# The last sequence chunk's bias in whole-array products, and the opening steps in an order written by hand

## The chip, the cores and the metric

One core of a Trainium2 chip runs the whole program in one launch. The metric is device time in microseconds (us) of an execution, the median of several; times of single steps come from one profiled execution. The engines are TensorE (PE, with its weight loads as PEld), VectorE (DVE), ScalarE (ACT), GpSimd (POOL) and SyncE (SP), which issues the transfers.

## The reference

Attention with a bias from a small network on relative positions, then an MLP with a squared ReLU (B = 4, H = 8, S = 576, D = 64, hidden 32):

```python
scores = scale * np.matmul(q, k.transpose(0, 1, 3, 2))
rel = (pos[:, None] - pos[None, :]).astype(np.float32)
psi_rel = np.log1p(np.abs(rel))
psi_i = np.log1p(np.maximum(pos[:, None].astype(np.float32), 1.0))
x = (psi_rel / psi_i)[..., None]
h = np.maximum(x @ w1 + b1, 0.0)
bias = h @ w2                                  # (S, S, H)
scores = scores + bias.transpose(2, 0, 1)[None]
attn = softmax(scores);  y = attn @ v          # (B, H, S, D)
x = y.transpose(0, 2, 1, 3).reshape(2304, 512)
g = np.maximum(x @ w_in, 0.0) ** 2
out = g @ w_out
```

## The kernel before, in words

**The bias.** It is the same for all batches. A hidden unit is either on or off, and for a row i it switches at one distance, theta[unit, i]. So a 0/1 mask (distance >= theta) is made by DVE for 32 hidden units by 4 positions on the 128 partitions, and a product with the small matrix `wmov` (w1*w2 and b1*w2, in two fp16 parts, scaled by a power of two) sums the units on PE. The result has a part to be multiplied by x (`xc`, on DVE) and a part to be added (scaled on ACT); POOL adds the two into `bias_t`, slices of the large tile `area`.

**Chunks.** The 576 rows are four chunks of 128 rows and a tail of 64 (`TAIL`, index 4). One head fills the partitions in a full chunk; in the tail, two heads share them, 64 rows each. The columns j come in blocks of 32 (`jb`, 18 of them). For a full chunk a block takes one mask of 128 x 8 x 128 and 16 products of 128 mask columns by 64 columns of `wmov` (L378). For the tail a block covers 64 columns of j: one mask holds the 64 rows for two neighbouring 32-column pieces, and 64 products of 64 mask columns by 32 columns (L397) put each head pair's half on its own partitions. There are nine such blocks.

**Opening.** The transfers of col (w1, b1, w2, psi of the tail), dist, psi, xc and the first keys, queries and values are issued by SP. PE runs 12 products of ones to warm up. `bias_scalars`, `bias_signs`, `bias_exp`, `bias_theta` make theta for the tail's 64 columns and for the main 512 with DVE steps, an exponential and a logarithm on ACT; `bias_weights` makes `wmov` on DVE, with one small product (pw) that finds the power of two. Then the tail's nine blocks follow, for which three mask buffers exist, and the loads of the further heads. The order of all this is chosen by a scheduler from a modelled timeline.

**Units.** The first 40 units (8 tail units, then 8 for each chunk) are pairs of heads of two batches: score products (L429), a DVE step that subtracts the bias and takes the minimum (L439), the exponential on ACT (L444), transposes, products with the values (L528). A line in that loop has the bias blocks for the next chunk done meanwhile, 20 of chunk 0's and the next one's by the eighth tail unit. This part is scheduled by the same planner; from unit 40 on, and in the MLP, the order is written by hand.

Of the kernel before, what the change touches and what calls it, by code (L numbers as in the profile page):

```python
# [77 lines left out]
def attention_then_relu2_mlp(ctx: ExitStack, tc: tile.TileContext, q, k, v, cols, w_in, w_out, psi, xmat, dist, out):  # L78
# [205 lines left out]
    def bias_scalars():  # L284
        ts = DVE.tensor_scalar
        ts(out=iz, in0=w1, scalar1=0.0, scalar2=None, op0=ALU.is_equal)
        DVE.tensor_tensor(out=den, in0=w1, in1=iz, op=ALU.add)
        DVE.reciprocal(out=den, in_=den)
        DVE.tensor_tensor(out=tt, in0=b1, in1=den, op=ALU.mult)
        ts(out=tt, in0=tt, scalar1=-1.0, scalar2=50.0, op0=ALU.mult, op1=ALU.min)  # L290
        ts(out=tt, in0=tt, scalar1=-50.0, scalar2=None, op0=ALU.max)

    def bias_signs():
        ts = DVE.tensor_scalar
        ts(out=pos, in0=w1, scalar1=0.0, scalar2=None, op0=ALU.is_gt)
# [5 lines left out]
        DVE.tensor_tensor(out=tmp, in0=tmp, in1=iz, op=ALU.mult)
        DVE.tensor_tensor(out=kk, in0=neg, in1=sg, op=ALU.subtract)
        DVE.tensor_tensor(out=kk, in0=kk, in1=tmp, op=ALU.add)

    def pin(ins):
        if PN:
            tc.keep_in_program_order(ins)
# [4 lines left out]
    def bias_exp(lo, hi):  # L312
        a = tha[:, lo:hi]
        DVE.tensor_scalar(out=a, in0=psi_of(lo, hi), scalar1=tt, scalar2=7.0, op0=ALU.mult, op1=ALU.min)
        pin(ACT.activation(out=a, in_=a, func=AF.Exp))

    def load_table(func):

        t = prep.tile([128, 1], F32, name="table", tag="table", bufs=1)
        pin(ACT.activation(out=t, in_=ones[:, :1], func=func))  # L320

    def bias_theta(lo, hi):
        ts = DVE.tensor_scalar
        p, a, n1 = psi_of(lo, hi), tha[:, lo:hi], thn[:, lo:hi]
        ts(out=n1, in0=a, scalar1=1.0, scalar2=MAGIC, op0=ALU.max, op1=ALU.add)
        ts(out=n1, in0=n1, scalar1=-MAGIC, scalar2=None, op0=ALU.add)
        pin(ACT.activation(out=a, in_=n1, func=AF.Ln))
        ts(out=a, in0=a, scalar1=w1, scalar2=None, op0=ALU.mult)
        DVE.scalar_tensor_tensor(out=a, in0=p, scalar=b1, in1=a, op0=ALU.mult, op1=ALU.add)
        ts(out=a, in0=a, scalar1=sg, scalar2=0.0, op0=ALU.mult, op1=ALU.is_lt)  # L330
        DVE.tensor_tensor(out=a, in0=a, in1=n1, op=ALU.add)
        ts(out=theta[:, lo:hi], in0=a, scalar1=sg, scalar2=kk, op0=ALU.mult, op1=ALU.add)

    def bias_weights():
        ab = prep.tile([128, 2, H], F32, name="ab")
        part = prep.tile([128, 2, 2 * H], F16, name="part")
        eng = POOL if BW else DVE
        eng.memset(wmov, 0.0)
        for n in range(2):
            eng.tensor_scalar(out=ab[:, n].rearrange("p (e h) -> p e h", e=2), in0=col[:, 2:10].rearrange("p (h e) -> p e h", e=2), scalar1=(w1, b1)[n], scalar2=8.0, op0=ALU.mult, op1=ALU.mult)  # L340
        r = ab.rearrange("p a h -> p (a h)")

        pw = bank("pw")
        sig, isig = power(r, pw[:, 0:1])
        eng.tensor_scalar(out=r, in0=r, scalar1=sig, scalar2=None, op0=ALU.mult)
        eng.tensor_copy(out=part[:, 0], in_=r)
        eng.tensor_tensor(out=part[:, 1], in0=r, in1=part[:, 0], op=ALU.subtract)
# [22 lines left out]
    def bias_sum(ic, jb):  # L370
        m = mask_t.pop((ic, jb))
        bb = bank("bb")
        t = prep.tile([128, H, 32], F32, name="bt1", tag="bt1", bufs=BB)
# [1 line left out]
        if ic < TAIL:
            for r in range(8):
                for n in range(2):
                    PE.matmul(bb[:, 64 * (7 - r):64 * (8 - r)], lhsT=m[:, r], rhs=wmov[:, n], start=(n == 0), stop=(n == 1))  # L378
            xv = xc_t[ic][:, 32 * jb:32 * jb + 32].rearrange("p (g j) -> p g j", j=4).unsqueeze(1)
            bv = bb.rearrange("p (g a h j) -> p a h g j", g=8, a=2, h=H)  # L380
            tv = t.rearrange("p h (g j) -> p h g j", j=4)
            sv = s.rearrange("p h (g j) -> p h g j", j=4)
            ACT.activation(out=sv, in_=bv[:, 1], func=AF.Identity, scale=bscale)
            DVE.tensor_tensor(out=tv, in0=bv[:, 0], in1=xv.to_broadcast([128, H, 8, 4]), op=ALU.mult)  # L384
            dst = bias_t[:, 2 * ic, 32 * jb:]
            odd = S + (64 if jb < 16 else -512)
            dst = bass.AP(tensor=dst.tensor, offset=dst.offset, ap=[dst.ap[0], [9 * S, HP], [odd, 2], [1, 32]])
            tw, sw = (y.rearrange("p (e h) j -> p h e j", e=2) for y in (t, s))
            POOL.tensor_tensor(out=dst, in0=tw, in1=sw, op=ALU.add)  # L389
        else:  # L390
            wv = wmov.rearrange("p n (a e y) -> p n e a y", a=2, e=2)
            for x in range(2):
                for r in range(8):
                    o = 256 * x + 32 * (7 - r)
                    for n in range(2):
                        for e in range(2):
                            PE.matmul(  # L397
                                bb[64 * e:64 * e + 64, o:o + 32].rearrange("p (a y) -> p a y", a=2),
                                lhsT=m[:, r, 64 - 64 * x:128 - 64 * x], rhs=wv[:, n, e], start=(n == 0), stop=(n == 1),
                            )  # L400
            xv = xc_t[ic][:, 32 * jb:32 * jb + 64].rearrange("p (g j) -> p g j", j=4).unsqueeze(1)
            bv = bb.rearrange("p (g a h j) -> p a h g j", g=16, a=2, h=HP)
            tv = t.rearrange("p (h x) y -> p h (x y)", x=2)
            sv = s.rearrange("p (h x) y -> p h (x y)", x=2)
            ACT.activation(out=sv.rearrange("p h (g j) -> p h g j", j=4), in_=bv[:, 1], func=AF.Identity, scale=bscale)
            DVE.tensor_tensor(out=tv.rearrange("p h (g j) -> p h g j", j=4), in0=bv[:, 0], in1=xv.to_broadcast([128, HP, 16, 4]), op=ALU.mult)
            POOL.tensor_tensor(out=bias_t[:, 8::9, 32 * jb:32 * jb + 64], in0=tv, in1=sv, op=ALU.add)
# [150 lines left out]
    for _ in range(WU):  # L558
        PE.matmul(warm[:, :128], lhsT=ones, rhs=ones, start=True, stop=True)
    bias_scalars()  # L560
    bias_exp(512, S)
    bias_signs()
    bscale = bias_weights()
    if E2:
        bias_exp(0, 512)
    load_table(AF.Ln)
    bias_theta(512, S)
    if E2 == 2:
        bias_theta(0, 512)
        load_table(AF.Exp)  # L570
    todo = [(ic, jb) for ic in chunks for jb in range(0, NJB, 2 if ic == TAIL else 1)]
    bias_mask(*todo[0])
# [10 lines left out]
    scale_xc(chunks[0])  # L583
    bias_upto(K0)
    for hp in range(1, HP):
        load_k(0, hp)
        load_q(0, hp)
        load_v(0, hp)
        bias_upto(B1[hp - 1])
        if hp == 1:  # L590
            load_xc(chunks[1])
            scale_xc(chunks[1])
# [657 lines left out]
```

## Time and profile before

| | us |
|---|---|
| median of 3 runs (741.26 to 742.96) | 741.63 |
| the profiled execution | 741.05 |
| its span | 739.2 |
| PE busy (96% of the span) | 708.7 |
| DVE busy (75%) | 552.8 |
| ACT busy (64%) | 472.0 |
| POOL busy (24%) | 180.3 |

Busy time is an average over stages that differ; what a change in one stage is worth is read from that stage. Starts are counted from the start of the span. In lines of instructions, x is the count, and the time behind "idle before" is what the engine stood still ahead of them, with what ended it.

### The profile page before, as it was taken

The page shows a single profiled execution, that of the slowest core. Times are in us where ns is not written, and L with a number is a line of the kernel's source. Part 1 is how long each engine was busy: PE and PEld are TensorE (multiplying, and loading weights), DVE is VectorE, ACT ScalarE, POOL GpSimd, SP SyncE. Part 2 cuts the span into 40 slices and gives each one's busy share as a digit, 9 for nine tenths or more (in the row PEclk, how much of TensorE's full clock was granted, in tenths as well). Part 3 has the DMA queues.
Part 4 walks back from the last instruction along what each step waited for, and adds up shares of the span by engine and source line. Part 5 has one row for each costly group of instructions (what it writes and reads, how often), then busy time and mean ns, then how long its engine had stood idle before and what let it go on. Part 6 is the DMA issues. An engine that isn't in the chain of part 4 may idle for free.

```text
span 739.2 us, 18203 instructions
## 1 busy us (share of the span) xinstructions
PE 708.7 (96%) x7382; PEld 573.4 (78%) x7382; DVE 552.8 (75%) x1186; ACT 472.0 (64%) x946; POOL 180.3 (24%) x289
## 2 busy tenths in 40 slices
PE   6889999999999999999999999999999999999992
PEld 5867877777777776777877888888888888888881
DVE  6599888885668889888898977868467775567661
ACT  4278787877767788888766747676466655455220
POOL 0464333332110047332532313212010112001000
PEclk7599999999999999999999999999999999999997
DMA  7630000002448422410442432150047312533100
GB/s 215 180 97 19 2 18 3 2 2 71 162 174 286 137 69 64 137 59 4 142 184 101 167 132 110 62 215 1 1 150 290 130 58 100 214 115 114 58 2 29
DMA packets 31608, 75.34 MB, mean 102 GB/s; under 512 B 5540, under 2 KB 13732, under 8 KB 30500
## 3 DMA queue, kind: packets, MB, share of 16 engines
q1 hardware_dynamic: 31524, 74.17, 29.0%
q8 instruction: 58, 0.95, 0.5%
q14 instruction: 26, 0.21, 0.1%
HBM read 55.81 MB, written 18.35 MB: 100 GB/s over the span
## 4 chain that ended last, share of the span: by engine, by line
PE 86%; DVE 8%; issue 2%; ACT 2%; DMA 0%; SPq 0%; ACTq 0%; DVEq 0%
PE y L1126 25%; PE ha L1031 12%; PE px L528 11%; PE sp L429 11%; PE hb L1031 9%; PE pp L509 9%; PE bb L378 4%; PE bb L397 2%; DVE mask L367 2%; PE pa L512 1%; DVE t L439 1%; ACT p L444 1%; PE ra L489 1%; ACT pt L966 1%; DVE bt L384 1%
## 5 line engine op out<-in xcount | busy, mean ns | idle before, releaser
L1031 PEld LDWEIGHTS <-area 128*128 128x128 f16 x1680 | 147.6, 98 | 24.9 <-issue 8.7
L1126 PE MATMUL y<-w,gh 128*128 128x512 f32 x576 | 149.1, 398 | 1.1 <-ACT gh L1070 1.1
L439 DVE CUSTOM_DVE_ANT_0 t<-sp,area 128x576 f32<-128x576 f32 x144 | 103.7, 753 | 28.7 <-PE sp L429 25.8
L1126 PEld LDWEIGHTS y<-w,gh 128*128 128x128 f32 x576 | 105.1, 188 | 23.2 <-ACT gh L1070 2.1
L444 ACT ACTIVATE p<-t,negm 128x576 f32<-128x576 f32 x144 | 111.8, 777 | 12.6 <-DVE negm L439 12.5
L429 PE MATMUL sp<-k,q 64*128 64x288 f32 (+1 forms) x640 | 100.4, 429 | 3.6 <-DMA q<-in_q 2.9
L528 PE MATMUL px<-pt,v 128*64 128x128 f32 (+1 forms) x1600 | 96.8, 267 | 1.8 <-DVE bt L384 1.2
L528 PEld LDWEIGHTS px<-pt,v 128*64 128x64 f32 x1600 | 79.2, 137 | 16.7 <-issue 6.4
L1031 PE MATMUL ha<-area 128*128 128x256 f16 (+1 forms) x816 | 85.4, 260 | 0.0
L509 PE MATMUL pp<-ident,p 128*128 128x128 f32 x576 | 82.2, 280 | 0.3 <-DVE xT L495 0.3
L1126 PE MATMUL y<-w,gl 128*128 128x512 f32 x288 | 79.0, 390 | 0.0
L509 PEld LDWEIGHTS pp<-ident,p 128*128 128x128 f32 x576 | 61.5, 141 | 19.5 <-issue 7.2
L389 POOL TENSOR_TENSOR area<-bt,bt 128x256 f32<-128x256 f32 x72 | 53.8, 770 | 73.5 <-DVE bt L384 73.5
L429 PEld LDWEIGHTS sp<-k,q 64*128 64x128 f32 (+1 forms) x640 | 53.3, 176 | 23.4 <-issue 7.5
L367 DVE TENSOR_TENSOR mask<-sdist,theta 128x1024 f16<-128x1024 f16 x81 | 55.7, 724 | 14.3 <-PE bb L397 8.1
L1031 PE MATMUL hb<-area 128*128 128x256 f16 (+1 forms) x612 | 64.9, 260 | 0.0
L1126 PEld LDWEIGHTS y<-w,gl 128*128 128x128 f32 x288 | 54.1, 188 | 12.2 <-DVE gl L1071 0.2
L966 ACT COPY pt<-pp 128x512 f32<-128x512 f32 x76 | 44.0, 579 | 27.6 <-PE pp L509 27.5
L781 ACT COPY pt<-pp 128x512 f32<-128x512 f32 x68 | 37.6, 588 | 14.1 <-PE pp L509 14.0
L1071 DVE TENSOR_TENSOR gl<-area,gh 128x512 fp32r<-128x512 f32 (+1 forms) x40 | 25.4, 669 | 26.0 <-ACT gh L1070 24.2
L1071 DVE TENSOR_TENSOR gl<-xT,gh 128x512 fp32r<-128x512 f32 (+1 forms) x36 | 25.5, 748 | 22.3 <-ACT gh L1070 20.7
L378 PEld LDWEIGHTS <-mask 128*128 128x128 f16 x1152 | 36.9, 100 | 5.4 <-issue 3.9
(164 smaller groups left out, 1020.8 us busy)
## 6 DMA issues: line engine op xcount, KB each, us to landing
raw<-in_w_in SPq DMA_DIRECT2D x32, 512.0 KB, 3.8
r<-in_w_out SPq DMA_DIRECT2D x16, 512.0 KB, 6.0
xs<-area SPq DMA_DIRECT2D x4, 1792.0 KB, 13.3
py<-o SPq DMA_DIRECT2D x12, 512.0 KB, 3.0
o<-py SPq DMA_DIRECT2D x12, 512.0 KB, 4.2
v<-in_v SPq DMA_DIRECT2D x16, 320.0 KB, 4.1
q<-in_q SPq DMA_DIRECT2D x32, 128.0 KB, 3.2
out<-o SPq DMA_DIRECT2D x8, 512.0 KB, 2.9
```

Source lines behind the costliest of these rows:

```text
L367: DVE.tensor_tensor(out=out, in0=win, in1=th, op=ALU.is_ge)
L378: PE.matmul(bb[:, 64 * (7 - r):64 * (8 - r)], lhsT=m[:, r], rhs=wmov[:, n], start=(n == 0), stop=(n == 1))
L389: POOL.tensor_tensor(out=dst, in0=tw, in1=sw, op=ALU.add)
L429: mm = PE.matmul(out_t[to, x, :HALF], lhsT=qt[rows, cols], rhs=kt[rows, k0:k0 + HALF], start=True, stop=True)
L439: DVE.tensor_tensor_reduce(out=t.rearrange("p (x n) -> p x n", x=2), in0=sp[:, :, :HALF], in1=bias.rearrange("p (x n) -> p x n", x=2), sca ...
L444: ACT.activation(out=p[:, S * n:S * n + S], in_=t, func=AF.Exp, bias=negm[:, n:n + 1], scale=-1.0, accum_out=sums[:, 2 * ic + n:2 * ic + n ...
L509: PE.transpose(pp[:, 128 * c:128 * c + 128], p[:, k0:k0 + 128], ident)
L528: PE.matmul(px[64 * h:64 * h + 64, :w], lhsT=vt[:, c, h], rhs=src, start=(c == 0), stop=(c == 4))
L966: ACT.copy(*c)
L1031: PE.matmul(h[:, s, :w], lhsT=a, rhs=x, start=(k == 0), stop=(k == 5))
L1071: DVE.tensor_tensor(out=gl, in0=g, in1=gh.bitcast(F32), op=ALU.subtract)
L1126: PE.matmul(y_t[n][k], lhsT=(gl if m == 2 else gh)[:, slot, o:o + 128], rhs=wl if m == 1 else wh, start=((n, P) in firsts and f == 0 and m ...
```

## The change

- A tail block is made as in the other chunks, 16 products of 128 mask columns by 64: the mask's two halves are the same 64 rows for columns 32*jb and for columns 288 further on. The nine blocks now cover 32 columns each in both halves. The sum goes to a piece of `area` (`tail_sum`) with the column half on the partition half.
- From there four copies for the first 160 columns (ACT) and four for the last 128 (ACT and DVE in turn) move 64 partitions by 4 heads each to the partitions that the softmax reads (`tail_bias`).
- The xc tile of the tail is loaded as two transfers of 64 rows by 288 columns.
- `wmov` is made on POOL. `bias_signs` is merged into `bias_scalars`.
- psi is the second transfer, dist the third.
- The opening stands in a block whose order is written by hand: 4 warm-up products, the weights, 8 more; the tail's theta ahead of the main one; three masks ahead of the products; unit 0's score products after the seventh block; the last four steps of the main theta, and the first mask of chunk 0, behind the last block.

```diff
     SP.dma_start(out=col, in_=cols)
+    SP.dma_start(out=psi_t, in_=psi)
     SP.dma_start(out=dist_t, in_=dist)
-    SP.dma_start(out=psi_t, in_=psi)
...
-            base = sdist[:, 128 * ic + 548 - 32 * (jb + 1):]
-            win = bass.AP(tensor=base.tensor, offset=base.offset, ap=[base.ap[0], [4, 8], [32, 2], [1, 64]])
+            base = sdist[:, 128 * ic + 548 - 32 * jb - HALF:]
+            win = bass.AP(tensor=base.tensor, offset=base.offset, ap=[base.ap[0], [4, 8], [HALF, 2], [1, 64]])
...
+        if ic == TAIL:
+            POOL.tensor_tensor(out=tail_sum[:, :, 32 * jb:32 * jb + 32], in0=t, in1=s, op=ALU.add)
+            return
...
+    def tail_bias(x, e, lo, hi, copy):
+        src = tail_sum[64 * x:64 * x + 64, HP * e:HP * e + HP, lo:hi]
+        copy(bias_t[64 * e:64 * e + 64, 8::9, HALF * (1 - x) + lo:HALF * (1 - x) + hi], src)
...
-        negm, sps = score_products(u)
+        negm, sps = begun.pop(u) if u in begun else score_products(u)
...
+    with tc.manual_schedule():
+        late, main = theta_steps(512, S), theta_steps(0, 512)
+        places = [(x, e) for x in range(2) for e in range(2)]
+        NT = NJB // 2
+        split = 32 * 5
+        warm_up(4)
+        weights_scaled()
+        bias_scalars()
+        late.pop(0)()
+        top = overall(ab_row)
+        pw = bank("pw")
+        PE.matmul(pw[:, 0:1], lhsT=ones, rhs=top, start=True, stop=True)
+        warm_up(8)
+        main.pop(0)()
+        late.pop(0)()
+        sig, bscale = power_of(pw[:, 0:1])
+        weights_spread(sig)
+        main.pop(0)()
+        load_table(AF.Exp)
+        DVE.tensor_scalar(out=sdist, in0=dist_t, scalar1=sg, scalar2=None, op0=ALU.mult)
+        for step in late:
+            step()
+        for jb in range(3):
+            bias_mask(TAIL, jb)
+        main.pop(0)()
+        scale_xc(TAIL)
+        for jb in range(NT):
+            bias_sum(TAIL, jb)
+            if jb + 3 < NT:
+                bias_mask(TAIL, jb + 3)
+            if jb == 6:
+                begun[0] = score_products(0, False)
+            if jb >= 5:
+                tail_bias(*places[jb - 5], 0, split, ACT.copy)
+        for step in main:
+            step()
+        bias_mask(*todo[0])
+        for m, spot in enumerate(places):
+            tail_bias(*spot, split, HALF, ACT.copy if m % 2 else DVE.tensor_copy)
+        for hp in range(1, HP):
+            load_k(0, hp)
+            load_q(0, hp)
+            load_v(0, hp)
+            if hp == 1:
+                load_xc(0)
+        scale_xc(0)
```

`theta_steps` returns, for its columns, seven steps: the exponential (a DVE step and ACT), the rounding and the logarithm (two DVE steps and ACT), and five single DVE steps.

## Rows read from the trace of the kernel before

**Rows 1.** Busy time by stage; then granted PE clock, DMA share, GB/s.
```profile
0.00:35.47 35.47, 25.96 (x664) 24.35 (x665) 21.58 (x71) 12.46 (x22) 9.67 (x20) 0.62 0.70 200
35.47:63.76 28.29, 25.66 (x452) 18.77 (x451) 25.72 (x54) 20.69 (x52) 18.36 (x27) 1.00 0.27 83
63.76:180.00 116.24, 116.24 (x1780) 92.24 (x1778) 93.28 (x234) 91.80 (x233) 39.22 (x59) 1.00 0.04 11
```

**Rows 2.** The chain of waits from 13 to 36 us, shares by line.
```profile
by line: PE bb L397 70.4%; issue 14.4%; DVE mask L367 6.4%; DVE wmov L350 2.6%; DVE t L439 2.4%; DVE bt L384 1.8%; DVE bt L406 1.8%; DVEq L367 0.1%; DVEq L384 0.1%
```

**Rows 3.** Lines by form, 0 to 35.47 us: busy us, mean ns | idle before.
```profile
L397 PE MATMUL bb<-wmov,mask 128*64 128x32 f16 x576 | 16.2, 214 | 5.5 <-issue 2.9 <-DVE wmov L350 2.7
...
L367 DVE TENSOR_TENSOR mask<-sdist,theta 128x1024 f16<-128x1024 f16 x14 | 9.8, 712 | 8.2 <-PE bb L397 8.1
L407 POOL TENSOR_TENSOR area<-bt,bt 128x256 f32<-128x256 f32 x9 | 7.7, 867 | 25.1 <-DVE bt L406 25.1
```

**Rows 4.** Timeline of the first 14 us: start, duration, engine, line.
```profile
1.72 0.20 POOL L553 TENSOR_TENSOR pick<-ident 27x9 bf16<-27x9 f32 x1
...
2.58 0.15 DVE L286 TENSOR_SCALAR sc<-col 128x1 f32<-128x1 f32 x1 [1.66 <-DMA col<-in_cols]
...
3.56 0.16 DVE L195 TENSOR_REDUCE small<-ab 128x1 f32<-128x16 f32 x1
4.01 0.52 DVE L298 TENSOR_SCALAR sdist<-area,sc 128x1152 f16<-128x1152 f16 x1 [0.29 <-DMA area<-in_dist]
...
6.21 1.28 ACT L327 ACT_TABLE_LOAD   x1
...
7.80 0.25 DVE L328 TENSOR_SCALAR area<-area,col 128x64 f32<-128x64 f32 x1 [1.08 <-ACT area L327]
...
8.76 2.25 PE L429 MATMUL sp<-k,q 64*64 64x288 f32 x8 [2.88 <-DMA q<-in_q]
...
10.60 1.89 DVE L367 TENSOR_TENSOR mask<-sdist,theta 128x1024 f16<-128x1024 f16 x3
...
13.67 0.51 PE L397 MATMUL bb<-wmov,mask 128*64 128x32 f16 x13 [2.65 <-DVE wmov L350]
```

**Rows 5.** Timeline of DVE in the tail's loop.
```profile
17.61 0.42 DVE L406 TENSOR_TENSOR bt<-bb,xc 128x256 f32<-128x256 f32 x1 [1.32 <-ACT bt L405]
17.95 0.68 DVE L367 TENSOR_TENSOR mask<-sdist,theta 128x1024 f16<-128x1024 f16 x1
```

**Rows 6.** Lines by form of DVE, 0 to 35.47 us, steps of 512 columns.
```profile
L329 DVE SCALAR_TENSOR_TENSOR area<-area,col 128x512 f32<-128x512 f32 x1 | 0.7, 745 | 0.0
L331 DVE TENSOR_TENSOR area<-area 128x512 f32<-128x512 f32 x1 | 0.7, 691 | 0.0
...
L330 DVE TENSOR_SCALAR area<-area,sc 128x512 f32<-128x512 f32 x1 | 0.5, 479 | 0.0
```

**Rows 7.** Lines by form, 35.47 to 63.76 us.
```profile
L367 DVE TENSOR_TENSOR mask<-sdist,theta 128x1024 f16<-128x1024 f16 x19 | 15.2, 835 | 0.9 <-PE bb L378 0.9
L378 PE MATMUL bb<-wmov,mask 128*128 128x64 f16 x271 | 9.7, 194 | 0.5 <-DVE bt L384 0.3 <-DVE mask L367 0.2
...
L781 ACT COPY pt<-pp 128x512 f32<-128x512 f32 x6 | 3.5, 582 | 0.3 <-PE pp L509 0.3
```

**Rows 8.** Timeline: first and ninth softmax step, last transfers issued, unit 7's scores.
```profile
35.47 0.75 DVE L439 CUSTOM_DVE_ANT_0 t<-sp,area 128x576 f32<-128x576 f32 x1
...
40.78 0.99 SPq L161 DMA_DIRECT2D q<-in_q  x1
...
58.63 1.19 PE L429 MATMUL sp<-k,q 64*64 64x288 f32 x8
...
63.76 0.76 DVE L439 CUSTOM_DVE_ANT_0 t<-sp,area 128x576 f32<-128x576 f32 x1
```

**Rows 9.** Busy time by stage, as rows 1: where the granted clock is low.
```profile
8.00:8.50 0.50, 0.00 (x0) 0.00 (x0) 0.50 (x4) 0.02 (x1) 0.00 (x0) 0.64 0.89 196
13.67:32.60 18.93, 16.07 (x576) 15.75 (x575) 9.54 (x18) 4.35 (x9) 6.57 (x8) 0.50 0.68 191
```

More of the change, by code (lines that the diff above doesn't have):

```diff
@@ L120, in attention_then_relu2_mlp @@
     SP.dma_start(out=col, in_=cols)
+    SP.dma_start(out=psi_t, in_=psi)
     SP.dma_start(out=dist_t, in_=dist)
-    SP.dma_start(out=psi_t, in_=psi)
     xc_t = {}
     def load_xc(ic):
-        xc_t[ic] = prep.tile([128, S], F32, name="xc", tag="xc", bufs=2)
-        SP.dma_start(out=xc_t[ic], in_=xmat[ic])
+        t = prep.tile([128, S], F32, name="xc", tag="xc", bufs=2)
+        if ic < TAIL:
+            SP.dma_start(out=t, in_=xmat[ic])
+        else:
+            t = t[:, :HALF]
+            for x in range(2):
+                rows = slice(64 * x, 64 * x + 64)
+                SP.dma_start(out=t[rows], in_=xmat[ic, rows, HALF * (1 - x):HALF * (2 - x)])
+        xc_t[ic] = t
     def scale_xc(ic):
@@ L284, in bias_scalars @@
     def bias_scalars():
-        ts = DVE.tensor_scalar
+        ts, tensor = DVE.tensor_scalar, DVE.tensor_tensor
         ts(out=iz, in0=w1, scalar1=0.0, scalar2=None, op0=ALU.is_equal)
[L287 to L291, printed above, removed]
@@ L293, in bias_signs @@
-    def bias_signs():
-        ts = DVE.tensor_scalar
         ts(out=pos, in0=w1, scalar1=0.0, scalar2=None, op0=ALU.is_gt)
         ts(out=neg, in0=w1, scalar1=0.0, scalar2=None, op0=ALU.is_lt)
-        DVE.tensor_tensor(out=sg, in0=pos, in1=neg, op=ALU.subtract)
-        DVE.tensor_scalar(out=sdist, in0=dist_t, scalar1=sg, scalar2=None, op0=ALU.mult)
+        tensor(out=den, in0=w1, in1=iz, op=ALU.add)
         ts(out=tmp, in0=b1, scalar1=0.0, scalar2=None, op0=ALU.is_gt)
+        tensor(out=sg, in0=pos, in1=neg, op=ALU.subtract)
@@ L300, in bias_signs @@
+        DVE.reciprocal(out=den, in_=den)
         ts(out=tmp, in0=tmp, scalar1=-2000.0, scalar2=1000.0, op0=ALU.mult, op1=ALU.add)
[L301 to L307, printed above, removed]
+        tensor(out=kk, in0=neg, in1=sg, op=ALU.subtract)
+        tensor(out=tt, in0=b1, in1=den, op=ALU.mult)
@@ L309, in psi_of, with theta_steps, exponent, distance @@
+        tensor(out=tmp, in0=tmp, in1=iz, op=ALU.mult)
+        ts(out=tt, in0=tt, scalar1=-1.0, scalar2=50.0, op0=ALU.mult, op1=ALU.min)
+        tensor(out=kk, in0=kk, in1=tmp, op=ALU.add)
+        ts(out=tt, in0=tt, scalar1=-50.0, scalar2=None, op0=ALU.max)
     def psi_of(lo, hi):
         return col[:, 10 + lo - 512:10 + hi - 512] if lo >= 512 else psi_t[:, lo:hi]
[L312 to L315, printed above, removed]
+    def theta_steps(lo, hi):
+        ts = DVE.tensor_scalar
+        p, a, n1 = psi_of(lo, hi), tha[:, lo:hi], thn[:, lo:hi]
+        def exponent():
+            ts(out=a, in0=p, scalar1=tt, scalar2=7.0, op0=ALU.mult, op1=ALU.min)
+            ACT.activation(out=a, in_=a, func=AF.Exp)
+        def distance():
+            ts(out=n1, in0=a, scalar1=1.0, scalar2=MAGIC, op0=ALU.max, op1=ALU.add)
+            ts(out=n1, in0=n1, scalar1=-MAGIC, scalar2=None, op0=ALU.add)
+            ACT.activation(out=a, in_=n1, func=AF.Ln)
+        return [
+            exponent, distance,
+            lambda: ts(out=a, in0=a, scalar1=w1, scalar2=None, op0=ALU.mult),
+            lambda: DVE.scalar_tensor_tensor(out=a, in0=p, scalar=b1, in1=a, op0=ALU.mult, op1=ALU.add),
+            lambda: ts(out=a, in0=a, scalar1=sg, scalar2=0.0, op0=ALU.mult, op1=ALU.is_lt),
+            lambda: DVE.tensor_tensor(out=a, in0=a, in1=n1, op=ALU.add),
+            lambda: ts(out=theta[:, lo:hi], in0=a, scalar1=sg, scalar2=kk, op0=ALU.mult, op1=ALU.add),
+        ]
@@ L317, in load_table @@
     def load_table(func):
         t = prep.tile([128, 1], F32, name="table", tag="table", bufs=1)
[L320 to L338, printed above, removed]
-        for n in range(2):
[L340 to L347, printed above, removed]
+        ACT.activation(out=t, in_=ones[:, :1], func=func)
@@ new lines, in attention_then_relu2_mlp, with weights_scaled, weights_spread @@
+    ab = prep.tile([128, 2, H], F32, name="ab")
+    part = prep.tile([128, 2, 2 * H], F16, name="part")
+    ab_row = ab.rearrange("p a h -> p (a h)")
+    def weights_scaled():
+        POOL.memset(wmov, 0.0)
+        for n in range(2):
+            POOL.tensor_scalar(out=ab[:, n].rearrange("p (e h) -> p e h", e=2), in0=col[:, 2:10].rearrange("p (h e) -> p e h", e=2), scalar1=(w1, b1)[n], scalar2=8.0, op0=ALU.mult, op1=ALU.mult)
+    def weights_spread(sig):
+        POOL.tensor_scalar(out=ab_row, in0=ab_row, scalar1=sig, scalar2=None, op0=ALU.mult)
+        POOL.tensor_copy(out=part[:, 0], in_=ab_row)
+        POOL.tensor_tensor(out=part[:, 1], in0=ab_row, in1=part[:, 0], op=ALU.subtract)
@@ L348, in bias_weights @@
         wv = wmov.rearrange("p n (m j) -> p n m j", j=4)
         for jj in range(4):
-            eng.tensor_copy(out=wv[32 * jj:32 * jj + 32, :, :, jj], in_=part[32 * jj:32 * jj + 32])
-        return isig
+            POOL.tensor_copy(out=wv[32 * jj:32 * jj + 32, :, :, jj], in_=part[32 * jj:32 * jj + 32])
     mask_t = {}
+    tail_sum = area[:, 29 * S:33 * S].rearrange("p (h j) -> p h j", h=H)
     def bias_mask(ic, jb):
@@ L374, in bias_sum @@
         s = prep.tile([128, H, 32], F32, name="bt2", tag="bt2", bufs=BB)
[L375 to L407, printed above, removed]
@@ new lines, in bias_sum @@
+        for r in range(8):
+            for n in range(2):
+                PE.matmul(bb[:, 64 * (7 - r):64 * (8 - r)], lhsT=m[:, r], rhs=wmov[:, n], start=(n == 0), stop=(n == 1))
+        xv = xc_t[ic][:, 32 * jb:32 * jb + 32].rearrange("p (g j) -> p g j", j=4).unsqueeze(1)
+        bv = bb.rearrange("p (g a h j) -> p a h g j", g=8, a=2, h=H)
+        tv = t.rearrange("p h (g j) -> p h g j", j=4)
+        sv = s.rearrange("p h (g j) -> p h g j", j=4)
+        ACT.activation(out=sv, in_=bv[:, 1], func=AF.Identity, scale=bscale)
@@ new lines, in bias_sum @@
+        DVE.tensor_tensor(out=tv, in0=bv[:, 0], in1=xv.to_broadcast([128, H, 8, 4]), op=ALU.mult)
+        if ic == TAIL:
+            POOL.tensor_tensor(out=tail_sum[:, :, 32 * jb:32 * jb + 32], in0=t, in1=s, op=ALU.add)
+            return
+        dst = bias_t[:, 2 * ic, 32 * jb:]
+        odd = S + (64 if jb < 16 else -512)
+        dst = bass.AP(tensor=dst.tensor, offset=dst.offset, ap=[dst.ap[0], [9 * S, HP], [odd, 2], [1, 32]])
+        tw, sw = (y.rearrange("p (e h) j -> p h e j", e=2) for y in (t, s))
@@ L410, in attention_then_relu2_mlp @@
+        POOL.tensor_tensor(out=dst, in0=tw, in1=sw, op=ALU.add)
+    def tail_bias(x, e, lo, hi, copy):
+        src = tail_sum[64 * x:64 * x + 64, HP * e:HP * e + HP, lo:hi]
+        copy(bias_t[64 * e:64 * e + 64, 8::9, HALF * (1 - x) + lo:HALF * (1 - x) + hi], src)
     p_t, pt_t, sum_t = {}, {}, {}
@@ L557, in attention_then_relu2_mlp, with warm_up @@
     warm = bank("warm")
[L558 to L572, printed above, removed]
+    def warm_up(n):
+        for _ in range(n):
+            PE.matmul(warm[:, :128], lhsT=ones, rhs=ones, start=True, stop=True)
+    todo = [(ic, jb) for ic in range(TAIL) for jb in range(NJB)]
     done = 0
@@ L581, in bias_upto @@
             done += 1
[L583 to L592, printed above, removed]
+    with tc.manual_schedule():
[44 more added lines that the diff above has]
+        scale_xc(0)
     for b in range(1, AB):
@@ L597, in attention_then_relu2_mlp @@
             load_v(b, hp)
-    if not E2:
-        bias_exp(0, 512)
-        load_table(AF.Ln)
-    if E2 < 2:
-        bias_theta(0, 512)
-        load_table(AF.Exp)
-    bias_upto(NJB // 2)
     wdst, xsig, alpha_t = {}, {}, {}
```

3 lines of the change are left out of this document (2 added, 1 removed).

## The prediction

> **What bounds the kernel now.** I read the stages first. From the first softmax subtraction of the first unit, at 35.47 us, to that of the ninth unit, at 63.76 [rows 8], VectorE (DVE) is busy 25.72 of 28.29 us and TensorE (PE) 25.66; from there to 180 us PE is busy without a gap; before 35.47 DVE has work for 21.58 us only [rows 1]. So the opening is a wait, the tail chunk's eight units are set by DVE and PE nearly equally, and the rest is PE's. A time saved ahead of 35.47 is kept to the end if the eight units don't give it back, since behind them the work is the same.
>
> What the opening waits for is in the chain of waits: 70.4% of 13 to 36 us is the tail's mask products (L397), 14.4% PE's own issue gaps [rows 2]. The grouped lines say the same from the other side: 576 products keep PE busy for 16.2 us, and DVE stands 8.2 us before its masks, all of it waiting for these products [rows 3]. They start only at 13.67, when DVE has made the weights (wmov); the masks stood ready from 10.60 on [rows 4].
>
> **The change, part by part.**
>
> *The products.* 576 of 64 mask columns by 32, 28 ns each at the half clock (16.2/576) [rows 3], become 9 x 16 = 144 of 128 by 64, the form that the other chunks use: 271 took 9.7 us at full clock, 36 ns each [rows 7]. At half clock I bound them by twice the old 28 (twice the columns): 56. A block costs 0.57 to 0.90 us instead of 1.80. A round of the loop costs DVE a product with xc, 0.34 to the next start, and a mask, 0.63 (three in 1.89) [rows 4, 5]: 0.97. So at either clock DVE becomes the pace of the loop, and the old wait of 8.2 us is gone.
>
> *The order of the first steps.* DVE starts at 2.58, when col lands, and 14 small steps take 1.14 us, 0.08 each (those at 2.58 and 3.56 are the first and the last) [rows 4]; 14 scalars are over at 3.7. psi is now the second transfer; the second one before, dist, held its reader until 4.01 [rows 4], so psi's first step runs 4.0 to 4.5 (0.48) [rows 6]. ScalarE (ACT): the exponential of 512, priced as its copy of 512, 0.58 [rows 7], to 5.1; the table load for the logarithm, 1.28 [rows 4], to 6.4; the logarithm of the 64 late columns, under the 0.58, I take 0.3: 6.7. Five DVE steps of 64 columns, at most 0.25 each [rows 4], end at 7.9. The main part's two rounding steps and sdist, some 0.5 each, fill DVE to 6.7 beside the table load. Three masks: 9.8. One 512-column step (0.48): 10.3.
>
> *Weights on POOL.* The power of two comes behind psi's step, two steps of 64 columns and four scalars on DVE, near 5.3; then seven small POOL steps, between 0.20 [rows 4] and 0.87 (the mean of its 256-column sum) [rows 3]; they are as small as the first, so I take 0.25: wmov at 7.1, and the first product waits for the mask, not for it. The cover lasts until the 10.3 less one block, 9.4; at 0.87 each, wmov would come at 11.4 and cost 2.0.
>
> *The loop.* Six rounds with a mask, 6 x 0.97 = 5.8, and three more xc products, 1.0: 17.1. In the seventh round PE also runs the eight score products of unit 0: 2.25 us at the half clock, 1.19 at full [rows 4, 8]. Queued behind them are the last two blocks, and DVE's next xc product waits for these; PE's slack takes part of it. Between nothing and 1.6 I take 0.9: 18.0.
>
> *What now stands behind the loop, on DVE.* Four 512-column steps, moved here: 0.745 + 0.691 + 2 x 0.48 = 2.4 [rows 6]; one mask 0.63; two copies of 64 partitions by 512 elements: between 0.25 and 0.69, I take 0.48 as for a 512-column step with one operand [rows 6]. That gives 22.0, with 0.5 for waits between engines 22.5. ACT's six copies (0.58 each and somewhat more for the longer four) [rows 7] start with the sixth block and end near 21 to 22, just covered; if they lag, each costs its 0.6. POOL's last sum of the tail must come before the second copies; the four DVE steps cover it.
>
> So the first softmax starts at 22.5 instead of 35.47, 13.0 earlier; bounds 21.4 and 25.
>
> *What the eight units then owe.* Before, 5 masks, 1 xc product and 54 mask products of chunk 0 were already done at 35.47 (14 masks of which 9 are the tail's [rows 3]); now one mask is. So 4 masks and 1 xc product come on top: the 19 masks of that stage took 0.835 each [rows 7], and DVE's operations overlap (I take 0.71 between starts): 4 x 0.71 + 0.34 = 3.2 us of DVE; 54 products more are 1.9 us of PE. The ninth unit's softmax: 22.5 + 28.3 + 3.2 = 54.0, against 63.76. **Saved: 9.8 us**, which leaves the idle 2.57 us of DVE in that stage [rows 1] as it was.
>
> *Loads.* The key, query and value transfers are no longer behind work. SyncE issues them in the same sequence, with one more for xc: the last query transfer was issued at 40.78, and unit 7's scores ran at 58.63 [rows 8]; they would now run near 49, some 8 us behind the issue. This covers it; a gain over some 13 us would meet it.
>
> **A rule weighed against a row.** While POOL's sums and DVE's masks run side by side, masks take 0.835 instead of 0.63 [rows 4, 7], so they do hinder each other. The Trainium skill ("SBUF — State Buffer", section "SBUF: two separate sides") says that the port pair which DVE and GpSimd share is an exclusive lock, so one would block the other for its whole length. By that the rounds of the new loop would last 0.63 + 0.87 = 1.50 us, and the sum would be 6.6 us saved instead of 9.8. The longer masks of the stage bear it out in part.
>
> **The rivals.**
> 1. *POOL and DVE in turn:* a round is a mask and then a sum of POOL, 0.63 + 0.87 [rows 3, 4]. Six rounds cost 0.53 more each, 3.2: saved 6.6, 735.0. For it the stretched masks; against it that in the old tail stage a mask started 0.34 after an xc product and lasted 0.68 [rows 5].
> 2. *The clock stays low, the side that ends slower.* PE stood idle for 2.88 us before 8.76, the granted clock fell to half at that time, and it stayed there for 19 us of products [rows 4, 9]. The new loop leaves PE idle in each round and for some 3 us before the first softmax. At half clock, PE's 27.6 us of the eight units (25.66 + 1.9) are 3.45 us a unit doubled, 6.9, against the 3.9 that DVE allows: each such unit costs 3.0. One unit: 734.8. From 3.3 units on nothing is left, and all eight would give 756. Against it: at the half clock PE would be busy without a break, and the clock was back at full for the whole stage [rows 1] where PE was busy 91%. The Trainium skill ("TensorE: Matmul & The Clock Gate", section "HAM oscillation — how this bites in real kernels") says that waits between bursts of products return the clock to its lower level each time; the fall at 8.76 agrees.
> 3. *The idle time goes too:* DVE saturated through the eight units, 2.57 more: 729.3.
> 4. *The transfers are the pace,* so that the products were hidden anyway: rows 8 speak against it by 8 us.
>
> **Numbers.** The profiled execution lasted 741.05 us, its span 739.2, 1.85 outside it; the median is 741.63, 0.6 above the execution. 739.2 - 9.8 = 729.4 of span; I take the difference from the median: 741.63 - 9.8 = 731.8. Chances: the forecast (730 to 733.5) 0.62; rival 3, 0.13; rival 1, 0.12; clock low for one or two units 0.06; slower by rival 2, 0.04; hidden or given back, no change, 0.03. A fifth of a per cent, 1.5 us, is about what a measurement here tells from nothing: faster 0.93, same 0.03, slower 0.04. The range takes in rivals 1 and 3 and one low unit, with the early and late bounds of 22.5: 728.8 to 736.
>
> **What would show it.** Mask products x144 at 36 to 56 ns; DVE nearly gapless from 7.9 to the first softmax between 21.4 and 25; the ninth unit's softmax between 51 and 57; PE without a gap behind it. Wrong would be: the first mask later than 9 (psi or a table), rounds of over 1.2 us (rival 1), the half clock behind 25 us (rival 2), or a ninth softmax not earlier than the first one's gain less 5 (the units give it back).

## The result

The changed kernel takes 733.17 us (median of 4 runs, 733.02 to 733.34), the kernel before 741.44 in the same job (739.7 to 742.96): ratio 0.9889, 95% interval 0.9867 to 0.9911, 8.3 us less (6.6 to 9.9 by the interval). The forecast was 731.8 in a range of 728.8 to 736. The profiled execution has a span of 731.3 us against 739.2, 7.9 less.

First the stages of the changed kernel by busy time (us; PE, PEld, DVE, ACT, POOL, then granted PE clock, DMA share, GB/s), cut where [rows 1] are cut: at the first and the ninth softmax step and 116 us on.

```profile
0.00:26.46 26.46, 16.07 (x203) 13.94 (x204) 20.88 (x59) 15.68 (x26) 13.55 (x29) 0.89 0.64 192
26.46:55.17 28.71, 27.81 (x479) 20.11 (x478) 26.59 (x57) 19.26 (x52) 18.09 (x27) 0.92 0.49 143
55.17:171.40 116.23, 116.23 (x1780) 92.24 (x1778) 93.27 (x234) 91.79 (x233) 39.19 (x59) 1.00 0.04 11
```

The opening is 9.0 us shorter with nearly the same DVE work (20.88 instead of 21.58): DVE's idle time fell from 13.9 to 5.6. The eight tail units take 28.71 instead of 28.29. Behind them PE is busy without a gap for the same 116.23, so what was won by then stays: the ninth softmax step is 8.59 earlier, and so is the 73rd. The remaining 0.7 went in three steps of 0.2 to 0.4 between the 73rd and the 140th softmax step.

The lines of the opening, by form (busy us, mean ns | idle before), which answer to [rows 3]:

```profile
L371 DVE TENSOR_TENSOR mask<-sdist,theta 128x1024 f16<-128x1024 f16 x12 | 9.0, 768 | 0.1
L381 PE MATMUL bb<-wmov,mask 128*128 128x64 f16 x169 | 8.9, 223 | 8.3 <-DVE mask L371 8.1
```

The wait has changed sides: DVE stood 8.2 us before its masks for PE; now PE stands 8.1 us for DVE's masks. 144 of the 169 products are the tail's, where there were 576.

The timeline of the changed kernel's opening, DVE, ACT, POOL and PE: the rounds, the end of the loop, and what follows it.

```profile
8.31 1.90 DVE L371 TENSOR_TENSOR mask<-sdist,theta 128x1024 f16<-128x1024 f16 x3
...
10.64 0.42 DVE L387 TENSOR_TENSOR bt<-bb,xc 128x256 f32<-128x256 f32 x1
...
11.21 6.73 POOL L389 TENSOR_TENSOR area<-bt,bt 128x256 f32<-128x256 f32 x6 [3.33 <-DVE bt L387]
...
15.01 0.41 DVE L387 TENSOR_TENSOR bt<-bb,xc 128x256 f32<-128x256 f32 x1
...
15.34 0.88 DVE L371 TENSOR_TENSOR mask<-sdist,theta 128x1024 f16<-128x1024 f16 x1
...
16.14 0.41 DVE L387 TENSOR_TENSOR bt<-bb,xc 128x256 f32<-128x256 f32 x1
...
16.84 0.72 ACT L399 COPY area<-area 64x640 f32<-64x640 f32 x1 [1.63 <-POOL area L389]
17.48 0.46 ACT L386 ACTIVATE bt<-bb,small 128x256 f32<-128x256 f32 x1
17.96 0.72 ACT L399 COPY area<-area 64x640 f32<-64x640 f32 x1
18.04 0.42 DVE L387 TENSOR_TENSOR bt<-bb,xc 128x256 f32<-128x256 f32 x1 [0.68 <-POOL area L389]
...
20.47 0.42 DVE L387 TENSOR_TENSOR bt<-bb,xc 128x256 f32<-128x256 f32 x1 [0.75 <-ACT bt L386]
...
20.81 0.74 DVE L327 SCALAR_TENSOR_TENSOR area<-area,col 128x512 f32<-128x512 f32 x1
...
23.76 0.69 DVE L371 TENSOR_TENSOR mask<-sdist,theta 128x1024 f16<-128x1024 f16 x1
...
24.37 0.85 DVE L399 COPY area<-area 64x512 f32<-64x512 f32 x2
24.50 0.88 PEld L381 LDWEIGHTS <-mask 128*128 128x128 f16 x16 [6.57 <-DVE mask L371]
...
25.25 1.29 DVE L371 TENSOR_TENSOR mask<-sdist,theta 128x1024 f16<-128x1024 f16 x2
```

Read it by the starts. From 15.01 to 16.14 a round takes 1.13 us, not 0.97; POOL's six sums follow one another without a gap, 1.12 each. From 16.84 on, ACT puts a copy between two of its scaled parts, and DVE's xc products come 1.2 us apart behind them. The first of these copies stands 1.63 us for POOL's fifth sum, and the scaled part of the seventh block stands behind it. PE stands still from 18 to 24.5. The planner sets two masks of chunk 0 ahead of the first softmax, which so starts at 26.46; the ninth starts at 55.17.

The granted clock, in the same columns as above:

```profile
10.00:18.00 8.00, 7.30 (x138) 5.96 (x135) 7.32 (x14) 3.98 (x9) 6.73 (x6) 1.00 0.66 195
18.00:22.00 4.00, 0.06 (x2) 0.00 (x0) 2.35 (x5) 3.08 (x5) 2.47 (x3) 0.83 0.67 204
...
24.50:30.00 5.50, 5.04 (x58) 3.44 (x59) 5.45 (x12) 2.07 (x5) 1.76 (x3) 0.50 0.76 234
...
31.00:36.00 5.00, 4.93 (x85) 3.25 (x82) 5.00 (x10) 4.10 (x11) 3.45 (x6) 1.00 0.63 186
```

In this execution the loop ran at full clock; the clock fell while PE stood still, the first units ran at half, and from 31 us on it was full again. DVE is busy for 5.45 of these 5.50 us all the same.

### The profile page after: what moved, and what is told of

It is laid out like the page before. It is cut to its first block, busy times and chain, and to the rows that moved or that the text cites. A ratio compares the mean times of both kernels' runs of the same rounds, so it can differ in the third digit from the quotient of the medians.

```text
span 731.3 us, 17344 instructions
## 1 busy us (share of the span) xinstructions
PE 700.7 (96%) x6950; PEld 564.6 (77%) x6950; DVE 553.2 (76%) x1178; ACT 474.0 (65%) x950; POOL 183.5 (25%) x299
## 4 chain that ended last, share of the span: by engine, by line
PE 86%; DVE 7%; ACT 3%; issue 2%; DMA 0%; ACTq 0%; DVEq 0%
PE y L1140 26%; PE ha L1045 12%; PE sp L421 11%; PE px L522 11%; PE hb L1045 9%; PE pp L503 9%; PE bb L381 5%; PE pa L506 1%; DVE t L431 1%; DVE mask L371 1%; ACT p L436 1%; ACT pt L980 1%; PE ra L483 1%; DVE wa L198 0%; DVE bt L387 0%
## 5 line engine op out<-in xcount | busy, mean ns | idle before, releaser
L503 PEld LDWEIGHTS pp<-ident,p 128*128 128x128 f32 x576 | 61.5, 141 | 18.9 <-issue 6.8
L381 PE MATMUL bb<-wmov,mask 128*128 128x64 f16 x1296 | 48.1, 199 | 9.1 <-DVE mask L371 8.1
L381 PEld LDWEIGHTS <-mask 128*128 128x128 f16 x1296 | 43.5, 102 | 16.0 <-DVE mask L371 10.2
```

Source lines behind the costliest of these rows:

```text
L503: PE.transpose(pp[:, 128 * c:128 * c + 128], p[:, k0:k0 + 128], ident)
```

## The experiments

Eleven kernels ran; landmarks are starts of DVE's softmax step in the profiled execution, times medians.

**Order alone.** The written order, the old products.

```diff
-            if jb >= 5:
-                tail_bias(*places[jb - 5], 0, split, ACT.copy)
...
-            bias_sum(TAIL, jb)
+            bias_sum(TAIL, 2 * jb)
```

with the mask, the xc transfer and the 64 products of the kernel before, and none of the copies.

> The hand-written opening with the old tail products (64 of 64 columns by 32 to a block, one xc transfer, no copies between partitions). Theory A, the form of the products is the larger part: 576 products start near 9 us instead of 13.7 and at 28 ns last to about 28, with the four late theta steps behind them the first softmax comes at 30 to 32, the ninth at 60 to 62, 2 to 4 us saved in all. Theory B, the order is the larger part: the first softmax by 28 and 5 us or more saved.

742.57 us against 741.28, ratio 1.0018 (1.0008 to 1.0027): nothing won, 0.18% lost. The first softmax starts at 29.59, 5.9 us earlier than before, the ninth 4.1 earlier; but by the 19th step the lead has fallen to 0.59, and at the end it is gone. PE of this kernel:

```profile
18.80 3.44 PE L380 MATMUL bb<-wmov,mask 128*64 128x32 f16 x123 [2.03 <-issue]
22.17 2.19 PE L431 MATMUL sp<-k,q 64*64 64x288 f32 x8
24.29 2.82 PE L380 MATMUL bb<-wmov,mask 128*64 128x32 f16 x128
...
72.82 0.66 PE L513 MATMUL pp<-ident,p 128*128 128x128 f32 x4 [0.73 <-ACT pt L801]
77.98 0.33 PE L516 MATMUL pa<-ident,p 128*128 128x128 f32 x1 [0.40 <-ACT pt L801]
```

The opening itself came out a little shorter than A said, and the total below A's: the early start shortened the opening, and chunk 0, whose order the planner makes anew, gave it back. From the ninth step to the 19th (59.65 to 83.88) PE is busy for 22.14 us and stands still for 2.1, where in the kernel before it is busy for all of 20.71; of the idle time 1.1 are the two waits above for ACT's copies of the transposes. So the lead of 4.1 at the ninth step also held work that PE still owed. Theory B falls. Why the planner chose that order was not tried.

**Products alone.** The kernel before with the new mask, products, xc transfers and copies.

```diff
     bias_upto(NJB // 2)
+    for spot in places:
+        tail_bias(*spot, 0, split, ACT.copy)
+    for m, spot in enumerate(places):
+        tail_bias(*spot, split, HALF, ACT.copy if m % 2 else DVE.tensor_copy)
```

> The old opening, ordered by the planner, with the new tail products, the two xc transfers and the copies. Theory A: products start near 13.7 us, nine rounds of 1.1 us and the copies put the first softmax at 26 to 29, 4.5 to 7 us saved in all. Theory B: less than 3.5 us saved, since the opening still starts late.

736.01 us, ratio 0.9932 (0.9918 to 0.9947): 5.3 less, as A says, though the first softmax starts at 32.1, later than A's 26 to 29, because the planner had masks and xc products of chunk 0 done ahead of it. The ninth is 5.3 earlier, and that stays. With -1.3 for the order and 5.3 for the products, the two together (8.3) are worth more than their sum. Why is not shown: the order alone lost its lead in chunk 0, in an order that the planner made for that kernel and not for this one.

**Copies behind the loop.**

```diff
-            if jb >= 5:
-                tail_bias(*places[jb - 5], 0, split, ACT.copy)
+        for spot in places:
+            tail_bias(*spot, 0, split, ACT.copy)
         for step in main:
```

> The changed kernel with the four first ACT copies behind the loop instead of between ACT's scaled copies of blocks 5 to 8. Theory C, ACT's queue sets the last three rounds (each xc product waits for ACT's scaled part, which waits behind a copy of 0.72 us): the last xc product starts near 18.9 instead of 20.47, the first softmax 1.3 to 1.8 us earlier, the ninth 0.5 to 1.5 earlier. Rival, POOL's sums set these rounds: the last xc product not earlier than 20.

730.37 us (730.21 to 732.77; the profiled execution is the one of 732.77). There the clock fell to half within the loop, so that the score products took 2.18 instead of 1.19, and DVE waited for the ACT part behind them:

```profile
15.94 2.18 PE L421 MATMUL sp<-k,q 64*64 64x288 f32 x8
18.06 1.29 PE L381 MATMUL bb<-wmov,mask 128*128 128x64 f16 x32
...
19.49 0.89 DVE L387 TENSOR_TENSOR bt<-bb,xc 128x256 f32<-128x256 f32 x2 [1.93 <-ACT bt L386]
```

The last xc product starts near 19.9, not at 18.9, and the first softmax is 0.3 earlier, below what theory C gave; the ninth is 0.76 earlier, within it. Not POOL, though: DVE's wait is for ACT's part, which waits for PE. That asks for the scores to be moved as well (below). The median is 2.8 less than the changed kernel's; the three executions that set it (730.21 to 730.52) have no trace, so where they win is open.

**POOL without reading.**

```diff
-            POOL.tensor_tensor(out=tail_sum[:, :, 32 * jb:32 * jb + 32], in0=t, in1=s, op=ALU.add)
+            POOL.memset(tail_sum[:, :, 32 * jb:32 * jb + 32], 0.0)
```

> The changed kernel with POOL writing zeros where it added the tail's two parts, so the tail has no bias; POOL then reads nothing in the loop. Theory D, a mask and POOL's sum hold one another up, which makes the round 1.13 us instead of the 0.97 that I summed: rounds of 0.95 to 1.0 and masks of 0.6 to 0.7 us. Rival, the longer masks come from something else (their three buffers, PE): rounds stay at 1.1 or more and masks at 0.88.

Rounds of 0.93 and masks of 0.68, from one xc product to the next; the last two xc products of the loop, and POOL's writes:

```profile
13.32 0.41 DVE L387 TENSOR_TENSOR bt<-bb,xc 128x256 f32<-128x256 f32 x1
13.66 0.68 DVE L371 TENSOR_TENSOR mask<-sdist,theta 128x1024 f16<-128x1024 f16 x1
14.26 0.41 DVE L387 TENSOR_TENSOR bt<-bb,xc 128x256 f32<-128x256 f32 x1
...
17.33 0.42 DVE L387 TENSOR_TENSOR bt<-bb,xc 128x256 f32<-128x256 f32 x1 [0.79 <-ACT bt L386]
18.58 0.42 DVE L387 TENSOR_TENSOR bt<-bb,xc 128x256 f32<-128x256 f32 x1 [0.82 <-ACT bt L386]
...
L389 POOL MEMSET area<- x9: 310/312/357, 7.9 to 10.0; 128x256 f32 x9
```

The first and the ninth softmax are both 2.2 us earlier than in the changed kernel, 730.65 us in one run. Theory D holds in that POOL's sums stretch the masks; the 0.97 that I summed is near what DVE needs alone. The edit did more than meant, though: the writes wait for nothing and were all over by 10.4, so POOL is idle beside the masks of the rounds, and these do not show what a step that only writes does. The three masks at 8.32, which ran beside the writes, do: 1.89 us, against 1.90 in the changed kernel, where POOL stood idle beside them. The last two xc products wait 0.79 and 0.82 for ACT's part with POOL idle, so ACT's queue holds them up, although the changed kernel's profile puts two of these waits down to POOL.

**POOL copying one operand.**

```diff
-            POOL.tensor_tensor(out=tail_sum[:, :, 32 * jb:32 * jb + 32], in0=t, in1=s, op=ALU.add)
+            POOL.tensor_copy(out=tail_sum[:, :, 32 * jb:32 * jb + 32], in_=s)
```

> The changed kernel with POOL copying the tail's added part alone (one operand read) where it summed two; the tail then lacks the part that xc multiplies. Theory D1, POOL's reading and DVE's masks hold one another up: rounds over 1.0 us though POOL's step is shorter alone. Theory D2, only the sum with two operands does: rounds of 0.93 as with zeros written.

POOL's step takes 0.40 and POOL stands idle for 0.7 us of each round, and yet the mask that starts beside it takes 0.87:

```profile
12.94 0.40 POOL L389 COPY area<-bt 128x256 f32<-128x256 f32 x1 [0.73 <-ACT bt L386]
...
12.68 0.41 DVE L387 TENSOR_TENSOR bt<-bb,xc 128x256 f32<-128x256 f32 x1
13.01 0.87 DVE L371 TENSOR_TENSOR mask<-sdist,theta 128x1024 f16<-128x1024 f16 x1
13.80 0.41 DVE L387 TENSOR_TENSOR bt<-bb,xc 128x256 f32<-128x256 f32 x1
...
16.41 0.67 DVE L371 TENSOR_TENSOR mask<-sdist,theta 128x1024 f16<-128x1024 f16 x1
16.64 0.71 POOL L389 COPY area<-bt 128x256 f32<-128x256 f32 x1 [1.03 <-ACT bt L386]
```

So it is D1: the mask is held up by a POOL step that reads, one operand or two, and not by how busy POOL is. It depends on which starts first: the mask at 16.41 had started when the copy came, and took 0.67, while the copy took 0.71. The clock too fell within the loop, which hides the gain at the later landmarks (26.45, 55.15; 732.92 us in one run).

**Idle PE filled.**

```diff
-    def warm_up(n):
+    def warm_up(n, warm=warm):
...
+        warm_up(24, bank("warm2"))
         for step in main:
             step()
```

> The changed kernel with 24 products of ones on the idle PE behind the last tail block, some 5.6 us, so that the granted clock is full where the units begin. Theory E, DVE sets the first units, so PE's half clock from 22 to 30 us costs nothing: first softmax and ninth softmax within 0.3 us of the changed kernel's 26.46 and 55.17, the time within 0.5 us. Rival, the half clock holds the first two units up (scores 2.19 instead of 1.19 us): the ninth softmax 1 to 2.5 us earlier.

The clock is full from the loop to the units, and the ninth softmax starts at 55.06, 0.11 earlier. The first one is 0.6 later than in the changed kernel because the planner put three masks ahead of it instead of two.

```profile
22.00:26.00 4.00, 2.17 (x30) 1.86 (x29) 3.85 (x8) 2.48 (x4) 0.17 (x1) 1.00 0.50 148
26.00:30.00 4.00, 3.68 (x73) 2.78 (x73) 4.00 (x9) 2.29 (x5) 1.73 (x3) 1.00 0.67 195
```

The changed kernel at its 75th softmax step:

```profile
198.75 1.09 PE L503 MATMUL pp<-ident,p 128*128 128x128 f32 x8 [0.76 <-DVE xT L489]
```

For the units theory E holds: DVE is as busy as before, and PE at half clock cost them nothing. The time is 732.32 (732.26 to 732.6), 0.85 less; 0.8 of it comes between the 73rd and the 77th softmax step, where the changed kernel's PE waits 0.76 us for DVE (xT) and this one does not wait. What moved that wait is open: it is gone too in the traces of the kernel with the copies behind the loop and of the one with eight products fewer (below), which fill nothing. The time missed the bound of 0.5 that I gave.

**Softmax of unit 0 in the written order.**

```diff
-        negm, sps = begun.pop(u) if u in begun else score_products(u)
+        if u in begun:
+            return
+        negm, sps = score_products(u)
...
             tail_bias(*spot, split, HALF, ACT.copy if m % 2 else DVE.tensor_copy)
+        softmax(0, 0, begun[0][0], begun[0][1][0])
```

> The changed kernel with the softmax step of unit 0 issued inside the hand-written order, right behind the copies, ahead of the two masks of chunk 0 that the planner put there. Theory F, what counts is DVE's total work, and the masks are owed anyway: the first softmax 1.2 us earlier (25.2), the ninth within 0.4 us of 55.17. Rival, the first softmax is the head of a chain through ACT and PE that the units wait for: the ninth is earlier by 0.8 us or more too.

The edit did not do what it was meant to: the two masks still stand ahead of the step on DVE, and it starts at 26.49:

```profile
25.28 1.29 DVE L371 TENSOR_TENSOR mask<-sdist,theta 128x1024 f16<-128x1024 f16 x2
26.49 0.75 DVE L431 CUSTOM_DVE_ANT_0 t<-sp,area 128x576 f32<-128x576 f32 x1
```

The ninth is 0.16 later, 733.24 us. The theories are not told apart.

**dist ahead of psi.**

```diff
     SP.dma_start(out=col, in_=cols)
-    SP.dma_start(out=psi_t, in_=psi)
     SP.dma_start(out=dist_t, in_=dist)
+    SP.dma_start(out=psi_t, in_=psi)
```

> The changed kernel with dist ahead of psi again. Theory G, psi's landing is on the chain of the opening (exponential, table, logarithm, theta): every step from psi's first on comes 0.4 to 0.6 us later, first mask near 8.8, ninth softmax 0.3 to 0.6 later. Rival, col and the scalars set it: no step moves by 0.2.

```profile
4.82 0.49 DVE L316 TENSOR_SCALAR area<-area,sc 128x512 f32<-128x512 f32 x1 [0.72 <-DMA area<-in_psi]
```

DVE waits 0.72 for psi, and everything is 0.75 later: first mask 9.08, first softmax 27.21, ninth 55.91. 734.05 us (733.85 to 734.24), 0.9 more. Theory G holds, with a larger size than I gave it. sdist, which reads dist, did not wait when dist came third.

**Scores and copies behind the loop.**

```diff
-            if jb == 6:
-                begun[0] = score_products(0, False)
-            if jb >= 5:
-                tail_bias(*places[jb - 5], 0, split, ACT.copy)
+        begun[0] = score_products(0, False)
+        for spot in places:
+            tail_bias(*spot, 0, split, ACT.copy)
```

> The changed kernel with both unit 0's score products and ACT's first four copies behind the loop. Theory C in its second form, the last three rounds wait for ACT's scaled part, which waits for a copy before it and for PE behind the score products: the last xc product near 18 instead of 20.47 (19.9 with the copies alone moved), the ninth softmax 1.5 to 2.5 us earlier than the changed kernel's, some 731. Rival, POOL's sums set the end of the opening (nine of 1.1 us from 11.1 on): the last copies wait for POOL near 21, and less than 1 us is won.

The last xc product starts at 18.63, the first softmax at 24.75, the ninth at 53.45, 1.72 earlier; 731.18 us (731.06 to 731.34), ratio 0.9867 to the kernel before. POOL has no gap in this opening, and ends at 20.4, ahead of DVE's last copies at 22.66:

```profile
11.20 9.23 POOL L389 TENSOR_TENSOR area<-bt,bt 128x256 f32<-128x256 f32 x9 [3.23 <-DVE bt L387]
```

Theory C holds in this form. In time this kernel is still 0.8 behind the one with the copies alone moved (730.37): its PE has the wait behind the 73rd step, and the traced execution of that one has not.

**The same with the idle PE filled.**

```diff
         begun[0] = score_products(0, False)
+        warm_up(16, bank("warm2"))
```

> Scores and copies behind the loop, and 16 products of ones behind the scores, so that PE does not stand still until chunk 0's first block. If the two effects seen apart add up (1.7 us at the ninth softmax from the moved steps, 0.1 there and 0.8 behind unit 72 with the idle PE filled), the time is 730.2 to 730.8; if the second was an accident of alignment, it stays at 731.2.

730.34 us (730.09 to 730.83), ratio 0.9852 (0.9839 to 0.9866): the time is what the two sum to, and below the kernel before and the changed one. That the second part is the filled PE's doing is not shown, since the copies alone moved, with nothing filled, give 730.37. In the profiled execution the clock fell to half within the loop, and the loop shows what that costs: three blocks in 3.31 us, 1.10 each instead of 0.64, and rounds that stay at 1.13 to 1.14 until the last two, which wait 0.23 and 0.71 for ACT's part.

```profile
15.37 3.31 PE L381 MATMUL bb<-wmov,mask 128*128 128x64 f16 x48 [0.28 <-DVE mask L371]
18.61 2.19 PE L421 MATMUL sp<-k,q 64*64 64x288 f32 x8
```

**Without the eight second warm-up products.**

```diff
-        warm_up(8)
         main.pop(0)()
```

> The changed kernel without the eight products of ones ahead of the tail's blocks, so that these may run at the half clock. My theory, the tail's loop is paced by DVE and POOL at either clock: blocks of 0.75 to 1.03 us instead of 0.64, rounds still 1.13, and only the score products (2.2 instead of 1.19) are late: the ninth softmax 0 to 1.2 us later. Rival, PE at half clock paces the loop: rounds of 1.2 or more.

```profile
9.04 5.78 PE L381 MATMUL bb<-wmov,mask 128*128 128x64 f16 x96 [4.32 <-DVE mask L371]
15.67 1.19 PE L421 MATMUL sp<-k,q 64*64 64x288 f32 x8
```

Inconclusive for its question: though PE stood still for 4.3 us ahead of the first block, the granted clock of this execution was 1.00 from 6 to 18 us, the scores took 1.19, and the ninth softmax stands at 55.12. Removing the products cost nothing in this one run (732.4 us; again without the wait behind the 73rd step). The kernel above answers the question in part: with its blocks at half clock the rounds stayed at 1.13 to 1.14.

## Why the prediction came out as it did

The mechanism was right: the products were what the opening waited for; with a quarter of them DVE paces the loop; the early start is kept behind the units. The size, 9.8 forecast and 8.3 measured, hides two terms that were off by more, in opposite directions: the first softmax came 4.0 later than summed, the units took 2.8 less. That these nearly cancel was luck. Nor does the time tell the forecast from rival 1, whose 6.6 lies about as near to 8.3, at the interval's other end; the rounds do.

*The first softmax: 26.46, not 22.5, past the late bound of 25.* Term by term, from the timeline above. The first mask came at 8.31 for 7.9, and the loop began at 10.64 for 10.3: the five 64-column steps, 0.23 to 0.31 long, start 0.26 to 0.34 apart, which costs 0.3 against the 0.25 each that I had at most. A block took 0.64 at the full clock, 40 ns a product for the 36 that I read, and at the half clock 1.10 (in the kernel with the idle PE filled last), 69 ns, above the 56 that I called a bound; neither made PE the pace. Six rounds took until 17.28 (16.14 and one more of 1.14), 6.64 us for 5.8: the step "a round costs DVE 0.97" failed by 0.17 in five of the six, 0.8 in all, and the two experiments on POOL show why. The last three xc products and the scores took until 20.81, 3.5 us for 1.9: I had put the delay on PE's score products alone (0.9), and called ACT's copies "just covered" by looking only at when they end. They stand in ACT's queue ahead of the scaled parts that the next xc products wait for. Moving both, the scores and the copies, won 1.7 at the ninth softmax. The four theta steps took 2.95 for 2.4, one of them 0.83 for 0.48 beside POOL's last sum; with POOL idle there the same step took 0.49. The mask and copies behind them were as forecast (1.49 for 1.59). And 1.2 us are the planner's two masks, where I had 0.5 for waits. Together 4.0.

*The units: 28.71, not 31.5.* Two of the four masks that I charged to them stood ahead of the first softmax, some 1.4. The 21 masks of that stage took 0.774 each, not 0.835:

```profile
L371 DVE TENSOR_TENSOR mask<-sdist,theta 128x1024 f16<-128x1024 f16 x21 | 15.6, 774 | 2.1 <-PE bb L381 2.0
```

which is some 1.1 us with the overlap that I reckoned. DVE's idle time is 2.12, against 2.57; rival 3 (it goes) didn't come. So of the four owed masks half only changed sides of the first softmax, and a landmark that the planner can move was a bad place to cut the sum. The ninth softmax, 55.17 for 54.0, was within its 51 to 57: 8.6 us won for 9.8. The last 0.7 between there and the end was not in the sum; it was lost in waits of 0.2 to 0.4 in the later units, and five of the kernels tried lack the first of them.

*Rival 1, POOL and DVE in turn.* Its mechanism is in the kernel, at a third of its price: rounds of 1.13, not 1.50, 0.16 above the forecast's and not 0.53. I had added POOL's mean step (0.87) whole to the mask, but that mean was itself stretched, and POOL's copy of one operand takes 0.40 with the mask 0.87. The lock of which the Trainium skill speaks ("SBUF — State Buffer", section "SBUF: two separate sides") agrees with the trace in kind: three masks beside steps that only write took as long as beside none (1.89 and 1.90), and a step that reads and starts ahead of the mask adds 0.2 to its 0.68, while a mask that had started first kept its 0.67. That one blocks the other for the whole recorded length the trace doesn't bear out: the copy overlaps 0.33 us of the mask and adds 0.2.

*Rival 2, the clock.* It fell as feared: it was half from 22 to 30 us, behind PE's idle stretch, which is one of the signs that I had named for being wrong. It cost next to nothing: with the clock kept full, the ninth softmax moved by 0.11. My price of 3.0 us a unit assumed that a unit at half clock is full of PE work; DVE was busy for 5.45 of 5.50 us instead, and the clock was full again from 31 us on, before the third softmax step at 33.09.

*Rival 4, the transfers,* never showed: in the changed kernel's trace no unit waits for keys, queries or values.

*The two halves of the change.* I reckoned the early start of wmov and the new products as one chain and did not ask what each is worth alone. The runs did: -1.3 and 5.3.

## What to carry over

When a stage is handed from one engine to another, sum the new pacer's steps at the length they have beside what will then run next to it, and follow each queue in order: a copy that ends early enough can still stand ahead of the step that others wait for. Cut a sum at a place that a planner cannot move (here the start of PE's gapless stretch), not at the first instruction of the next stage. And an earlier start was worth nothing by itself here, where the order behind it is made anew; run each half of a change alone. A wait far behind an edit can come or go with it, as the 0.8 us behind the 73rd step did: compare variants at the place that the edit was to move, and not by the end alone.

## What the runs showed of the hardware

- A DVE mask (two operands in SBUF, 128 x 1024, 16 bit) takes 0.68 us beside an idle POOL and 0.87 beside a POOL copy of 128 x 256 that lasts 0.40 and starts 0.07 ahead of it. Where the mask starts first, by 0.23, it takes 0.67 and the copy 0.71. Beside sums of two operands, POOL's sum goes from 0.72 to 1.12 and the mask to 0.88. Three masks beside POOL steps that only write take 1.89, as beside none (1.90).
- A transfer of 256 KB issued third instead of second, behind one of 288 KB, held its reader for 0.72 us, where it had not waited.
- The granted clock does not follow the program alone. With PE idle for 4.3 us ahead of the tail's blocks it stayed full through the loop in one execution; with 0.7 to 1.3 us it fell to half within the loop in three others with the new products (copies behind the loop, POOL copying, scores and copies late with PE filled). The kernels with the copies behind the loop and with scores and copies behind it have the same instructions up to 15 us, within 0.15 us of one another; the clock fell near 15 in the one, and stayed full to 22 in the other.
